# Loads of the down product's weights and of the logits' x placed later in the gate and up stage, and the head's first low parts in another order

## The chip, the cores and the metric

The kernel runs on one core of one Trainium2 chip. The metric is the time of an execution on the device, in microseconds (us). Before the change the median of three runs is 1020.63 us, and the three lie between 1020.56 and 1021.0. The profile comes from one further execution, which took 1021.83 us by itself; the span that the profile shows, from its first instruction to its last, is 1020.0 us.

## The reference

With x of 2048 positions and 640 features, all in 32-bit floats, the kernel computes two sublayers and mixes them by a gate per position:

```python
g = sigmoid((x * gate_w).sum(-1, keepdims=True))          # gate_w: 640
a = x @ dft_hid_re.T                                        # hidden DFT, 640 x 640
b = x @ dft_hid_im.T
y = dft_seq_re @ a - dft_seq_im @ b                         # sequence DFT, 2048 x 2048
ffn = (gelu(x @ w_gate) * (x @ w_up)) @ w_down              # F = 1728 hidden columns
out = g * y + (1 - g) * ffn
```

The arguments of the sigmoid, one per position, are called the logits below.

## The kernel before

**Products.** Every product of 32-bit floats is done as three matmuls of a shorter format: high x high, high x low and low x high (`mm3`, lines 101 to 103). For these ACT writes the high part of an operand (`high`, line 82) and DVE the low part as raw minus high (`low`, line 85). In the profile a name that ends in h or l is such a part. Most matrix products are also done blockwise: 2 x 2 blocks with seven products in place of eight, by sums of blocks of both operands. The sums of the weights are called S1 to S4, those of x T1 to T4.

**Stages.** The work goes through these stages, in this order:

- the *head*: the first 128 hidden columns (f = 0) and the 64 that are left over from 1728 = 13 x 128 + 64 ("m"), while x comes in piece by piece;
- the *gate and up stage*: twelve chunks of 128 hidden columns, f = 1 to 12, for which gelu(x w_gate) * (x w_up) is computed. "Chunk f" below is one turn of this loop;
- the *down stage*, the product with w_down, and behind it the sequence DFT, and last the hidden DFT with the gating.

**A chunk of the gate and up stage.** `gate_up` does a chunk's products for each half of the tokens. From chunk 3 on, two chunks make a pair: the odd one (3, 5, 7, 9, 11; kind 1 in the code) also does products that it shares with the even one behind it (kind 2), by a further level of blocks (`together` and `together_up`). The odd chunks take 30 us or more for this reason, the even ones some 17.6. `together` reads sums of x called T1 to T3, which were computed once and kept in memory; the loads that fetch them again for chunk f are called xq. `together_up` reads another such set, and its loads are called xu. Both are issued on POOL's queue (`load_across`, line 1150), the xu of an odd chunk within its first two steps, the xq in the fifth step of the chunk before. The gelu's results are stored to memory as blocks (hA) and sums of blocks (hT) by POOL (`keep`, line 404). In the odd chunks from 5 on, POOL also makes two of the weights' low parts, by a DMA that adds onto what stands in the buffer (`left_of`, line 97).

**Weights of the chunk.** Raw weights of chunk f + 2 are loaded in step 5 of chunk f (`load_w`). Their sums and parts for chunk f + 1 are made by work items of `make_w`: wa are the parts of the weights themselves, ws those of the sums of the chunk's own two columns of blocks, wq those of the sums across a pair. `make_up` makes the weights wu of `together_up` (its raw buffer is wu7r in chunk 7, its parts wu7h and wu7l).

**Two side works of the stage.** The first is the sums of w_down for the down stage: `sum_wd(k)` (line 606) loads a chunk's blocks as dr (512 KB) and da (128 KB) on SP's queue, makes four sums on DVE in two work items (lines 595 and 596, then 599 and 600) and stores them as wsd on SP's queue, behind the second item. Only the down stage reads wsd. The second is the logits: `load_z` (line 709) loads a tile of x, 128 positions by 640 features, as xz (320 KB, line 716), and a work item called a *total* multiplies it by gwb, the gate's weights, and sums it into one column of z on DVE (line 720). There are sixteen such tiles; the others are done elsewhere in the kernel. The gates of the first half of the tokens are made at chunk 12.

**What sets the order.** PE, ACT, DVE and POOL run the stage in exactly the order in which the host code emits the instructions (`in_order`). PE's steps are emitted as generators' steps, and the work of the other engines stands in one list, `fills`, of pairs (cost, function). After each step of PE the list is served so far as the spent costs stay within 1.25 times PE's share of the chunk:

```python
while fills and not (some and not fills[0][0]) and state["done"] <= 1.25 * state["all"] * state["pe"] / state["pe_all"]:
```

What is left is emitted at the end of the chunk. So the place of an item in `fills` and the costs ahead of it say when its instructions come on their engine. An engine that waits holds up all that stands behind it in its order. SP, which issues loads and a few stores, is not in this list of four engines, but its queue is served in its own order too.

**Buffers.** Most operands of the stage live in 46 equal buffers of one pool (tag s4, 4 KB on each of 128 partitions): weights raw and in parts, xq and xu, xz, dr, the gelu's blocks s. A new tile takes the buffer that has stood unused longest in the order of the code, and whoever fills it waits until the one who had it last is read out.

**Where the work stands before.** At the start of each odd chunk 5, 7, 9 and 11, right behind the loads of `make_up`, the code loads dr and da for a sum_wd and an xz; the two items of the sums stand early in the list, then follow a total in the middle, with it a second xz load, and a second total near the end; `make_w`'s items for the next chunk come last. In the even chunks 6 and 8 (`ZE_AT`) one xz is loaded at the start, and its total is the item at place 5. Chunk 3 (`PAIRED`) has a sum_wd and no total, chunk 12 a sum_wd of its own.

**The head.** For the first 128 rows of the contraction (d = 0) x's first piece x011 comes in two halves of 256 columns, and so do its parts and its products with the left-over columns' weights (w0h and w0l in the profile, wh and wl in the code, line 1051). PE, ACT and DVE are held in the code's order here as well.

Of the kernel before, what the change touches and what calls it, by code (L numbers as in the profile page):

```python
# [22 lines left out]
NF = F // P  # L23
# [4 lines left out]
EORD = [0, 2, 1, 3, 4]  # L28
PAIRED = 3
ZB_AT = [5,7,9,14,15,16]  # L30
ZE_AT = [6, 8]
XB_DOWN = [17, 18]
XB_AT = [1, 3, 4, 5, 9, 10]
WU_AT = [4, 17, 19, 33, 35]
# [3 lines left out]
def kernel(  # L38
# [45 lines left out]
    def low(hi, lo, raw):  # L84
        nc.vector.tensor_tensor(lo, raw, hi.bitcast(F32), op=ALU.subtract)  # L85
# [910 lines left out]
    halves = [slice(0, T // 2), slice(T // 2, T)]  # L996
# [22 lines left out]
    with in_order(ACT, DVE, PE):  # L1019
        nc.scalar.activation(table, table, AF.Gelu_apprx_tanh)  # L1020
        idle = bank("idle")
        for k in range(14):
            nc.tensor.matmul(idle[:, halves[k % 2]], *ones, start=k == 0, stop=True, skip_group_check=True)
        bk1, bk2 = first_banks(0, 1), first_banks(0, 2)
        for d in range(ND):
            raw, _, (h, l) = piece(d, 1)
            first, *rest = FIRST[d]
            parts(high, *first)
            if d == 0:
                a, b = halves  # L1030
                nc.vector.tensor_copy(h[:, a], raw[:, a])
                parts(low, *first)
                low(h[:, a], l[:, a], raw[:, a])
                split(h[:, b], l[:, b], raw[:, b])
                parts(high, *rest[0])
                parts(low, *rest[0])
            else:
                high(h, raw)
                parts(low, *first)
                low(h, l, raw)  # L1040
                for r in rest:
                    parts(high, *r)
                for r in rest:
                    parts(low, *r)
            split_piece(d, 2)
            if d == 0:
                wh, wl = W0["m"][0]
                for c in halves:
                    for k, (w, x) in enumerate(((wh, h), (wl, h), (wh, l))):
                        first = k == 0 and c is halves[0]  # L1050
                        nc.tensor.matmul(bk1["m"][:, c], w, x[:, c], start=first, stop=False, skip_group_check=True)
                for n in "gu":
                    mm3(bk1[n], W0[n][0], (h, l), True, False)
            else:
                first_products(bk1, W0, B, 1, [d])
            first_products(bk2, W0, B, 2, [d])
        B0, (tsum0, his0, lows0) = B, (tsum, his, lows)
        Bs.append(B)
        B, tiles, load, piece, tsum, his, lows = load_x(1)
        tiles(1)  # L1060
        load(1)
        tiles(2)
        load(2)
        tsum0(1)
        his((1, 1), (2, 1))
        lows((1, 1), (2, 1))
        split_piece(4, 1)
        first_out(bk1, 0, 1)
        first_out(bk2, 0, 2)
        bk1 = first_banks(1, 1)  # L1070
        first_products(bk1, W0, B, 1)
        tsum0(3)
        his0("T1", "T3")
        lows0("T1", "T3")
        tsum0(2)
        tsum0(4)
        his((1, 2), (2, 2))
        lows((1, 2), (2, 2))
        split_piece(4, 2)
        his0("T2", "T4")  # L1080
        lows0("T2", "T4")
        first_out(bk1, 1, 1)
        load_w(1)
        W, work = make_w(1)
        for _, do in work:
            do()
        load_w(2)
        nc.sync.dma_start(gwb, gw.to_broadcast([P, D]))
        bk2 = first_banks(1, 2)
        first_products(bk2, W0, B, 2)  # L1090
        tsum(1)
        his("T1")
        tsum(2)
        his("T2")
        lows("T1")
        first_out(bk2, 1, 2)

        todo.extend([(114, partial(lows, "T2")), (114, partial(tsum, 3)), (0, partial(his, "T3"))])
        todo.extend([(114, partial(tsum, 4)), (0, partial(his, "T4"))])
        todo.extend([(114, partial(lows, "T3")), (114, partial(lows, "T4"))])  # L1100
# [52 lines left out]
    fills, state = deque(), {}  # L1153
# [15 lines left out]
            fill(ns)  # L1169
            next(steps)  # L1170

    s1t, s4 = {}, {}
    Tp.update(B11=at(Bs[0][2, 1], 0), B21=at(Bs[0][2, 1], 1), B22=at(Bs[1][2, 1], 1))
    blocks = [("11", xt[0, 2]), ("12", xt[2, 2]), ("22", xt[2, 3]), ("21", xt[0, 3])]
    keptp, loadp, t123, t4 = sums_across("xp", Tp, blocks, lambda: at(Bs[1][2, 1], 0))
# [2 lines left out]
    with in_order(PE, ACT, DVE, POOL):  # L1178
        for f in range(1, NF):
            kind = pair_of(f)  # L1180
# [5 lines left out]
            if kind == 1:  # L1186
                up, work = make_up(f, load_up(f))
                fills.extend(work)
            if kind == 1:
                lw, *w = sum_wd((f - PAIRED) // 2)  # L1190
                lw[1]()
                fills.extend(w)
            if f == PAIRED - 1:
                loadp()
                fills.extend(t123)
# [6 lines left out]
                if kind != 1 or f == PAIRED:  # L1202
                    fills.extend(work)
            if kind == 1 and f > PAIRED:
                (_, first), z1, (_, second), z2 = load_z(2)
                first()
                k = len(fills) // 2
                more = list(fills)
                fills.clear()
                fills.extend([*more[:k], z1, (0, second), *more[k:], z2, *work])  # L1210
            elif f in ZE_AT:
                (_, first), z1 = load_z(1)
                first()
                fills.insert(5, z1)
            if f == NF - 1:
                load_k(0)
                fills.extend(split_pieces(0))
# [481 lines left out]
```

## Time and profile before

| of the profile before | |
| --- | --- |
| median of three runs (lowest, highest) | 1020.63 us (1020.56, 1021.0) |
| the profiled execution's own time | 1021.83 us |
| its span | 1020.0 us |
| PE busy | 1015.6 us, 4483 matmuls |
| PEld busy | 840.2 us |
| DVE busy | 823.2 us |
| ACT busy | 486.1 us |
| POOL busy | 166.9 us |
| DMA, mean over the span | 262 GB/s |
| granted clock of TensorE | 1.0 |

PE is TensorE's matmuls, PEld its weight loads, which run beside the matmuls; DVE is VectorE, ACT ScalarE, POOL GpSimd, SP SyncE. A row of a timeline gives the start in us from the span's start, the length of the instruction, the engine (SPq is a load or store on SP's queue), the line of the code, the operation, what it writes and what it reads, the shapes, and in square brackets how long the engine stood before it and what released it. A row of the windows gives a stretch, its length, the busy time of PE, PEld, DVE, ACT and POOL with the number of instructions, and then the granted clock, the share of time in which the DMA engines were busy, and their GB/s. "To landing" is the time from the issue of a DMA to its end.

The chunks of the gate and up stage start on PE at these times of the profiled execution: chunk 3 at 95.4 us, 4 at 125.6, 5 at 143.2, 6 at 173.2, 7 at 190.85, 8 at 221.4, 9 at 239, 10 at 269.1, 11 at 286.7, 12 at 316.8, and the stage ends at 334.3.

### The profile page before, as it was taken

Reading aid. Unit: us, or ns where it says so; the run is one execution under the profiler, and the core shown is the slowest. Engines: PE = TensorE matmul, PEld = TensorE weight load, DVE = VectorE, ACT = ScalarE, POOL = GpSimd, SP = SyncE. Lnnn points to the kernel's source line nnn. Section 1 sums busy time; section 2 is a strip of 40 time slices with the busy share of each in tenths; the row PEclk is TensorE's granted clock in tenths of the full one; section 3 lists DMA queues with packets and bytes.
Section 4 is the critical chain, followed back from the end, with each engine's and each line's share of the span. In section 5 each row is a group of like instructions: output and inputs, shape, how many; then the busy total and the mean of one; then the engine's idle time right before and its main releaser. Section 6 shows DMA issues by size and latency. Waiting matters only on the chain.

```text
span 1020.0 us, 13269 instructions
## 1 busy us (share of the span) xinstructions
PE 1015.6 (100%) x4483; PEld 840.2 (82%) x4483; DVE 823.2 (81%) x1154; ACT 486.1 (48%) x622; POOL 166.9 (16%) x295
## 2 busy tenths in 40 slices
PE   9999999999999999999999999999999999999998
PEld 7888888888888888888888888888888888888887
DVE  6987877787787989888887976898588869797796
ACT  5544534353535667557444443444344444455440
POOL 0122242323231200100001012102210200021112
PEclk9999999999999999999999999999999999999999
DMA  7468588968699999979874669668866877897856
GB/s 271 168 209 276 181 264 275 314 225 290 201 315 313 415 374 383 330 245 329 295 254 172 213 223 337 223 200 298 302 203 209 294 252 275 295 349 215 274 134 99
DMA packets 96644, 267.58 MB, mean 262 GB/s; under 512 B 12672, under 2 KB 27008, under 8 KB 96576
## 3 DMA queue, kind: packets, MB, share of 16 engines
q1 hardware_dynamic: 70512, 185.24, 53.2%
q0 software_dynamic: 25776, 81.30, 24.4%
q8 instruction: 35, 0.57, 0.2%
q14 instruction: 33, 0.27, 0.1%
q10 hardware_dynamic: 288, 0.20, 0.1%
HBM read 192.48 MB, written 70.27 MB: 258 GB/s over the span
## 4 chain that ended last, share of the span: by engine, by line
PE 97%; issue 1%; DMA 1%; DVE 0%; POOL 0%; POOLq 0%
PE pX L103 6%; PE pX L102 6%; PE pX L101 6%; PE pZ L103 4%; PE pZ L102 4%; PE pZ L101 4%; PE pL L102 3%; PE pL L103 3%; PE pL L101 3%; PE pV L102 2%; PE pV L103 2%; PE pV L101 2%; PE pY L102 1%; PE pR L103 1%; PE pQ L101 1%; PE pQ L102 1%
## 5 line engine op out<-in xcount | busy, mean ns | idle before, releaser
L82 ACT ACTIVATE ch<-csa 128x1024 fp32r<-128x1024 f32 x32 | 34.0, 1063 | 78.2 <-DVE csa L770 76.7
L85 DVE TENSOR_TENSOR cl<-cra,ch 128x1024 fp32r<-128x1024 f32 x32 | 39.1, 1222 | 24.6 <-ACT ch L82 22.5
L82 ACT ACTIVATE ch<-cra 128x1024 fp32r<-128x1024 f32 x32 | 33.9, 1059 | 52.3 <-DVE cl L85 19.3
L85 DVE TENSOR_TENSOR cl<-crb,ch 128x1024 fp32r<-128x1024 f32 x32 | 39.1, 1223 | 14.4 <-ACT ch L82 14.4
L102 PE MATMUL pL<-cl,xah 128*128 128x512 f32 x128 | 49.9, 390 | 0.0
L103 PE MATMUL pL<-ch,xal 128*128 128x512 f32 x128 | 49.9, 390 | 0.0
L101 PE MATMUL pL<-ch,xah 128*128 128x512 f32 x128 | 49.7, 390 | 0.0
L82 ACT ACTIVATE ch<-crb 128x1024 fp32r<-128x1024 f32 x32 | 33.8, 1055 | 31.2 <-PE pL L102 11.4
L404 POOL DMA_DIRECT2D hA<-s x48 | 26.1, 544 | 132.7 <-DVE s L562 113.1
L85 DVE TENSOR_TENSOR cl<-csb,ch 128x1024 fp32r<-128x1024 f32 x32 | 39.2, 1225 | 3.7 <-ACT ch L82 2.3
L85 DVE TENSOR_TENSOR cl<-csa,ch 128x1024 fp32r<-128x1024 f32 x32 | 39.1, 1221 | 2.1 <-ACT ch L82 1.1
L82 ACT ACTIVATE ch<-csb 128x1024 fp32r<-128x1024 f32 x32 | 34.0, 1062 | 11.7 <-DVE csb L773 4.7
L556 ACT ACTIVATE s<-s 128x512 f32<-128x512 f32 x24 | 15.2, 633 | 46.7 <-DVE s L555 46.7
L148 ACT ACTIVATE s<-pX 128x512 f32<-128x512 f32 x40 | 23.5, 598 | 23.7 <-PE pX L103 22.4
L85 DVE TENSOR_TENSOR kl<-kw,kh 128x1024 fp32r<-128x1024 f32 x24 | 29.4, 1223 | 4.5 <-DMA kw<-in_wd 2.6
L82 ACT ACTIVATE kh<-kw 128x1024 fp32r<-128x1024 f32 x24 | 25.3, 1052 | 16.1 <-PE kR L103 6.2
L551 DVE TENSOR_TENSOR s<-s,pX 128x512 f32<-128x512 f32 x24 | 16.5, 686 | 19.6 <-PE pX L103 14.3
L1346 POOL DMA_DIRECT2D uA<-c x8 | 4.3, 542 | 168.9 <-DVE c L1448 168.7
L404 POOL DMA_DIRECT2D hT<-s x48 | 26.0, 541 | 24.3 <-DVE s L579 8.1
L929 POOL DMA_DIRECT2D out<-ks x12 | 6.5, 541 | 136.8 <-DVE ks L928 136.2
L101 PEld LDWEIGHTS pL<-ch,xah 128*128 128x128 f32 x128 | 24.0, 188 | 5.0
L102 PEld LDWEIGHTS pL<-cl,xah 128*128 128x128 f32 x128 | 24.0, 188 | 5.0
(3612 smaller groups left out, 3483.8 us busy)
## 6 DMA issues: line engine op xcount, KB each, us to landing
cra<-in_ct SPq DMA_DIRECT2D x64, 512.0 KB, 4.6
crb<-in_ct SPq DMA_DIRECT2D x64, 512.0 KB, 5.0
hA<-s POOLq DMA_DIRECT2D x48, 256.0 KB, 5.9
hT<-s POOLq DMA_DIRECT2D x48, 256.0 KB, 5.7
kr<-hA SPq DMA_DIRECT2D x24, 512.0 KB, 7.7
kr<-hT SPq DMA_DIRECT2D x24, 512.0 KB, 6.8
ux<-uA SPq DMA_DIRECT2D x24, 512.0 KB, 5.9
ux<-uT SPq DMA_DIRECT2D x16, 512.0 KB, 6.7
```

Of the source, the lines that this page charges most:

```text
L82: nc.scalar.activation(hi, raw, AF.Copy)
L85: nc.vector.tensor_tensor(lo, raw, hi.bitcast(F32), op=ALU.subtract)
L101: nc.tensor.matmul(ps, lh, rh, start=first, stop=False, skip_group_check=True)
L102: nc.tensor.matmul(ps, lh, rl, start=False, stop=False, skip_group_check=True)
L103: nc.tensor.matmul(ps, ll, rh, start=False, stop=last, skip_group_check=True)
L148: nc.scalar.activation(m, src, AF.Copy)
L404: nc.gpsimd.dma_start(to[:, i], src)
L551: tt(s5, s5, X, op=ALU.add)
L556: nc.scalar.activation(s2, s2, AF.Gelu_apprx_tanh)
L929: nc.gpsimd.dma_start(acc4[:, t] if tp and e == 4 else out[2 * tp + t, e], src)
L1346: nc.gpsimd.dma_start(to[:, i], src)
```

## The change

It has three parts.

- **The sums of w_down.** In chunks 5, 7, 9 and 11 the loads of dr and da no longer stand at the chunk's start; the load is now an item of cost 0 in `fills`, behind what stood there and ahead of `make_w`'s items, and the two items of the sums stand behind the first five of `make_w`'s. Chunks 3 and 12 stay as they are.
- **The logits.** The odd chunks 5, 7, 9 and 11 load no xz at their start and do no total. Each even chunk 4, 6, 8 and 10 loads two xz at its start, with their totals put into the list at places 9 and 12. Chunks 7 and 9 (`ZE_AT` now) issue one further xz load at the end of their list, and its total is put at place 4 of the list of the chunk behind, 8 and 10. So the even chunks have 2, 2, 3 and 3 totals, and the sum stays at ten.
- **The head.** For d = 0, DVE makes the low part of the first half of x ahead of the first weights' low part, and PE does the products of that half in the order (high, high), (weights high, x low), (weights low, x high). The second half's order stays.

```diff
-ZE_AT = [6, 8]
+ZE_AT = (7, 9)
@@ head, d == 0 @@
                 nc.vector.tensor_copy(h[:, a], raw[:, a])
+                low(h[:, a], l[:, a], raw[:, a])
                 parts(low, *first)
-                low(h[:, a], l[:, a], raw[:, a])
                 split(h[:, b], l[:, b], raw[:, b])
...
                 for c in halves:
-                    for k, (w, x) in enumerate(((wh, h), (wl, h), (wh, l))):
+                    order = ((wh, h), (wl, h), (wh, l)) if c is halves[1] else ((wh, h), (wh, l), (wl, h))
+                    for k, (w, x) in enumerate(order):
                         first = k == 0 and c is halves[0]
                         nc.tensor.matmul(bk1["m"][:, c], w, x[:, c], start=first, stop=False, skip_group_check=True)
@@ gate and up stage @@
-    s1t, s4 = {}, {}
+    s1t, s4, zlate = {}, {}, []
...
             if kind == 1:
                 lw, *w = sum_wd((f - PAIRED) // 2)
-                lw[1]()
-                fills.extend(w)
+                if f == PAIRED:
+                    lw[1]()
+                    fills.extend(w)
...
             if kind == 1 and f > PAIRED:
-                (_, first), z1, (_, second), z2 = load_z(2)
-                first()
-                k = len(fills) // 2
-                more = list(fills)
-                fills.clear()
-                fills.extend([*more[:k], z1, (0, second), *more[k:], z2, *work])
-            elif f in ZE_AT:
-                (_, first), z1 = load_z(1)
-                first()
-                fills.insert(5, z1)
+                fills.extend([lw, *work[:5], *w, *work[5:]])
+                if f in ZE_AT:
+                    fetch, z1 = load_z(1)
+                    fills.append(fetch)
+                    zlate.append(z1)
+            elif kind == 2 and f < NF - 1:
+                if zlate:
+                    fills.insert(4, zlate.pop())
+                for k in (9, 12):
+                    (_, do), z1 = load_z(1)
+                    do()
+                    fills.insert(k, z1)
```

## The prediction

> **What bounds the kernel now.** I read the page's span and busy rows first, then the engines' busy time by windows, then the chain of waits in order of time for the places where it leaves TensorE, and last the timelines around the one such place that the change touches. The page:
>
> ```profile
> span 1020.0 us, 13269 instructions
> PE 1015.6 (100%) x4483; PEld 840.2 (82%) x4483; DVE 823.2 (81%) x1154; ACT 486.1 (48%) x622; POOL 166.9 (16%) x295
> ```
>
> Busy time by windows (the window, its length, then the busy time of PE, PEld, DVE, ACT and POOL):
>
> ```profile
> 0.00:10.00 10.00, 9.22 (x37) 6.97 (x38) 4.02 (x10) 5.24 (x10) 0.20 (x4) 1.00 0.82 256
> 190.00:240.00 50.00, 49.88 (x220) 40.84 (x219) 37.88 (x74) 22.25 (x37) 14.22 (x25) 1.00 0.79 262
> 940.00:1020.00 80.00, 76.48 (x349) 63.69 (x347) 64.38 (x86) 26.50 (x31) 12.74 (x15) 1.00 0.71 175
> ```
>
> PE is the bound. It idles 0.78 us in the first window, 0.12 in the second and 3.52 in the last, around its last matmul; these three are the whole 4.4 us between span and busy time. So what a new order of loads can gain is capped at PE's few late starts, while a new wait of PE costs its full length. The one late start in the gate and up stage, in the chain of waits and on PE's timeline:
>
> ```profile
> 207.69 5.28 DMA xu<-xv
> 213.01 0.50 PE pH7u L101
> ```
>
> ```profile
> 212.27 0.39 PE L102 MATMUL pX<-xT03l,ws7h 128*128 128x512 f32 x1
> 212.50 0.39 PE L103 MATMUL pX<-xT03h,ws7l 128*128 128x512 f32 x1
> 213.01 0.50 PE L101 MATMUL pH7u<-xu,wu7h 128*128 128x512 f32 x1
> 213.34 0.40 PE L102 MATMUL pH7u<-xu,wu7h 128*128 128x512 f32 x1
> ```
>
> Undisturbed matmuls start 0.23 us apart (212.27 to 212.50). The start at 213.01 comes 0.51 after the one before it, and the next 0.33 after that: 0.28 + 0.10 = 0.38 us lost in chunk 7, because its second xu load (the kept sum T2) landed only then, 207.69 + 5.28 = 212.97. Why it was issued so late, on POOL, on DVE and on SP's queue:
>
> ```profile
> 202.58 0.55 POOL L1150 DMA_DIRECT2D xu<-xv  x1 [0.30 <-issue]
> 207.69 1.14 POOL L1150 DMA_DIRECT2D xu<-xv  x2 [4.56 <-DVE dr L595]
> ```
>
> ```profile
> 202.20 0.83 DVE L720 CUSTOM_DVE_ANT_0 xz<-xz,gwb 128x640 f32<-128x640 f32 x1 [3.64 <-DMA hT<-s]
> ...
> 206.46 0.82 DVE L85 TENSOR_TENSOR wu7l<-wu7r,wu7h 128x640 fp32r<-128x640 f32 x1 [0.57 <-DMA hT<-s]
> 207.20 0.42 DVE L595 TENSOR_TENSOR dr<-da,dr 128x256 f32<-128x256 f32 x1
> ```
>
> ```profile
> 191.04 0.62 SPq L612 DMA_DIRECT2D dr<-in_wd  x1
> 192.44 3.05 SPq L716 DMA_DIRECT2D xz<-in_xz  x2
> ```
>
> POOL was ready for this load at 203.1 and stood 4.56 us: the load takes over the buffer of wu7r, which DVE reads until 207.28 (206.46 + 0.82). The row names dr's sum as the releaser, but that had only begun at 207.20; the wu7l just ahead of it is what ends in time. DVE was late in turn, because it had stood 3.64 us in front of the total of an xz, and 0.57 us for a buffer that an hT store still held. The DMA view of 190.8 to 204 us, and one row of the same view for 125.6 to 143 us, where SP loads little:
>
> ```profile
> DMA packets 1737, 4.91 MB, mean 372 GB/s; under 512 B 253, under 2 KB 509, under 8 KB 1736
> ...
> hT<-s POOLq DMA_DIRECT2D x6, 256.0 KB, 7.6
> ...
> xz<-in_xz SPq DMA_DIRECT2D x2, 320.0 KB, 9.2
> dr<-in_wd SPq DMA_DIRECT2D x1, 512.0 KB, 8.3
> ```
>
> ```profile
> hT<-s POOLq DMA_DIRECT2D x2, 256.0 KB, 2.4
> ```
>
> The start of chunk 7 is thus a queue of transfers: a store that lands in 2.4 us elsewhere takes 7.6 here, an xz 9.2.
>
> **The change part by part.** *Chunks 5, 7, 9 and 11, their start.* SP no longer loads dr (512 KB) and two xz (320 KB each) there: 1152 KB or 1.18 MB, at 372 GB/s 3.2 us of transfer that the stores and xu no longer queue behind. Both totals leave DVE's order in these chunks. Without the 3.64 us, and without the 0.57 us (with two or three fewer takers ahead of it wu7l gets a buffer that came free earlier), wu7l starts at 206.46 - 4.21 = 202.25 and ends at 203.1, just when POOL comes to the load. How long xu takes, in the view of that tile:
>
> ```profile
> L1150 POOL DMA_DIRECT2D xu<-xv x12: 537/548/551, 154.6 to 302.6; - x12
> ...
>   DVE dr L595: 12.9, 3
> ...
> DMA to landing us min/median/max: 5.2/5.6/6.4
> ```
>
> At the longest, 6.4, T2 lands at 209.5, 3.5 us before PE wants it. The three waits of 12.9 us in all are those of POOL in chunks 5, 7 and 9; only the one in chunk 7 reached PE. The gain is 0.38 us, with ends of 0 (something else is late) and 0.38. I take 0.38, since 3.5 us of margin stand behind it.
>
> *Chunks 4, 6, 8 and 10.* They hold 2, 2, 3 and 3 totals where 0, 1, 1 and 0 stood. DVE's idle stretches in these four, in their order:
>
> ```profile
> 136.98 0.29 DVE L85 TENSOR_TENSOR wd<-wb,wd 128x128 fp32r<-128x128 f32 x1 [3.31 <-ACT wd L82]
> ...
> 185.68 0.69 DVE L551 TENSOR_TENSOR s<-s,pX 128x512 f32<-128x512 f32 x1 [1.65 <-ACT s L547]
> ...
> 233.81 0.69 DVE L551 TENSOR_TENSOR s<-s,pX 128x512 f32<-128x512 f32 x1 [3.58 <-ACT s L547]
> ...
> 280.47 0.29 DVE L85 TENSOR_TENSOR wd<-wb,wd 128x128 fp32r<-128x128 f32 x1 [3.31 <-ACT wd L82]
> ```
>
> A total takes DVE 0.83 us (the row at 202.20). What is added is 1.66, 0.83, 1.66 and 2.49 us against 3.31, 1.65, 3.58 and 3.31 idle, and these stretches lie behind the places where the totals go in: cost 0, covered by that idle time; were it gone, DVE would be late with ws of the next chunk by as much. A total must not stand for its landing. By the code's budget the totals come 8.2 to 10.2 us into the chunk, their loads at its start, so at the slowest landing (9.2) DVE stands about 1 us, which the same idle time takes up; the third xz of chunks 8 and 10 goes out at the end of the chunk before. What can suffer is the chain to xq, the T1 with which the next chunk opens; chunk 6 is the tightest:
>
> ```profile
> 185.39 0.57 POOL L1150 DMA_DIRECT2D xq<-xp  x1 [2.08 <-DMA wa7l<-wa7r]
> ...
> 191.53 0.39 PE L101 MATMUL pZ7t<-xq,wq7h 128*128 128x512 f32 x1
> ```
>
> ```profile
> DMA to landing us min/median/max: 3.8/5.0/7.0
> ```
>
> 185.39 + 5.0 leaves 1.1 us; at 7.0 PE would wait 0.9. One more xz is 0.9 us of transfer at 372 GB/s. The ends are 0 and 0.9; I take 0, as the xz go out some 12 us ahead of xq.
>
> A rule that speaks against this part: the Trainium skill, SBUF — State Buffer, section "Who interferes with whom", says that a vector instruction with both inputs in SBUF and a GpSimd one that reads SBUF exclude each other for the whole of whichever began first. If that holds for the descriptors of POOL's DMAs, totals beside its accumulating DMAs delay these, and the sum would be that of the third rival. The trace does not bear it out: the xu issue at 202.58 lay wholly beside a total (202.20 to 203.03) and took 0.55, as did the median of the twelve, 0.548; so by the row the sum stays.
>
> *The weights' sums in chunks 5, 7, 9 and 11.* The code's budget (costs of 1103 in all, spent at 1.25 times PE's share of the chunk) takes up dr's load 12.9 us into the chunk and its sums at 19.0 and 21.8; SP sends the load as soon as its buffer is free. What the buffer may wait for, and the matmul that DVE's sums may hold up:
>
> ```profile
> 207.06 1.08 ACT L537 ACTIVATE s<-pZ 128x512 f32<-128x512 f32 x2 [1.67 <-DMA hT<-s]
> ```
>
> ```profile
> 219.26 0.39 PE L101 MATMUL pH7u<-xT14h,wu7h 128*128 128x512 f32 x1
> ```
>
> The buffer is free at the latest with the last hT store, about 207.0; with the slowest dr, 8.3, it lands at 215.3. Until then DVE stands at the first sum. Queued behind it are the other three sums of 0.42 and three additions of 0.69 (two of pX, one of pH7u), after which PE may overwrite pH7u at 219.26: 4 x 0.42 + 3 x 0.69 = 3.75, so 219.05. The worst case just fits, by 0.2 us. With the stores up to 3.2 us sooner and 5.6 us for the load (the median of xu, of the same size) dr is there at 209.4, and the sums' place, 190.85 + 19.0 = 209.9 (chunk 7 starts one matmul group, 0.68 us, ahead of the 191.53 above), is not held up. Cost 0; what comes beyond is the slower rival. On SP the four wsd stores follow the sums, and the loads of chunk 9's weights stand behind them; chunk 8 lies between, so some us of delay are covered, and wsd is read only in the down stage. Cost 0.
>
> *Head.* x's first low half no longer stands behind w's low part on DVE, and PE takes it second in the first half.
>
> ```profile
> 3.69 0.58 PE L1051 MATMUL pm<-x011h,w0h 128*128 128x256 f32 x1
> ...
> 4.73 0.42 PE L1051 MATMUL pm<-x011h,w0h 128*128 128x256 f32 x1
> ...
> 7.64 0.51 PE L102 MATMUL pm<-x012l,w0h 128*128 128x512 f32 x1
> ```
>
> ```profile
> 6.23 0.63 ACT L82 ACTIVATE x012h<-xr 128x512 fp32r<-128x512 f32 x1 [1.76 <-DMA xr<-in_xt]
> ```
>
> The first half's three products take 1.04 us (3.69 to 4.73); the overlap of DVE's two parts could shorten that by the 0.29 to 0.38 that one of them takes, I estimate 0.3. But at 7.64 PE starts on the low part of x012, whose chain begins with a landing at 6.23 that the change does not touch (0.63 for the high part, then DVE's low part). What is won ahead is waited for there: 0, with 0.3 as the other end; I take 0, as the wait ends in a transfer.
>
> **Sum.** -0.38 us: span 1019.6, and this execution, 1021.83, becomes 1021.45. It lies 1.2 us above the median of the runs, to which the difference applies as well: 1020.63 - 0.38 = 1020.25. PE has no idle time between chunk 7 and its last matmul, so the gain is carried to the end whole.
>
> **The rivals.** (1) The stall stays, or one of its size takes its place: T2's buffer or POOL is late for another reason. For it: POOL works in strict order behind ten stores, and PE has little slack in these chunks. Against: 3.5 us of margin. 1020.6. (2) xq is late in chunk 6, up to +0.9: 1021.15. For: 1.1 us of margin and one xz more; against: those 12 us. (3) The totals hold POOL's accumulating DMAs: two in chunk 6, 1.66 - 1.1 = 0.6, and three in chunk 10, taken with the same margin, 2.49 - 1.1 = 1.4; +2.0, 1022.25. Against: the 0.55 of the row. (4) Slower: dr is late. From a landing past 215.5 in chunk 7 on DVE, and with it PE, is held us for us, and likewise in 5, 9 and 11; with one us past that point in each it is +4, 1024.25. For: these loads are given their buffers in turn, and the turn now comes after stores' buffers. Against: it takes the slowest store and the slowest load seen, with 1.18 MB less ahead of them. (5) The head's 0.3 comes through: 1019.95.
>
> **How the numbers follow.** The forecast has 0.63, the rivals 0.13, 0.11, 0.03, 0.07 and 0.03. About 0.2%, 2 us, is what a measurement of this kernel can tell from no change; only (4) lies beyond, and no case reaches 1018.6; for what I have not seen 0.01 stands there. So slower 0.07, within 0.92, faster 0.01. The range holds the forecast, (1), (2) and (5) with the 0.4 us by which the runs shown differ: 1019.8 to 1021.3; (3) and (4) are left out.
>
> **What would show it.** Right: pH7u starts 0.23 us after the matmul before it; the second xu of chunk 7 goes out near 203 to 205; the hT stores at the start of chunks 5, 7, 9 and 11 land in 5 us or less; at the head a longer gap ahead of 7.64. Wrong: DVE stands in front of dr's sum (L595) until dr lands and PE waits at pH7u; or PE waits at pZ7t for xq; or the second xu goes out at 207 as before.

## The result, and the profile after

The changed kernel takes 1022.10 us in the median of 22 executions (1020.63 to 1029.34), the kernel before 1021.11 (1020.45 to 1022.62, 22 executions). The ratio is 1.0021 with a 95% interval of 1.0012 to 1.0030: about 0.2% slower, where 0.04% faster was forecast. The forecast of 1020.25 stood on a median of three executions, 1020.63; over 22 the kernel before is at 1021.11, so 0.48 us of the distance come from that base and the rest from the change, 0.99 us slower in place of 0.38 faster. The spread says more than the median. None of these 22 executions of the kernel before lies above 1023; of the changed kernel eight in 22 do, and all eight lie between 1024.5 and 1029.3. Six of the eight show a mean granted clock of 0.996 to 0.998 in place of 1.0.

The profile shown was taken of an execution of 1021.19 us, on the fast side. The page:

```profile
span 1019.4 us, 13283 instructions
PE 1014.5 (100%) x4483; PEld 839.0 (82%) x4483; DVE 822.8 (81%) x1154; ACT 487.2 (48%) x622; POOL 167.2 (16%) x295
```

Busy time by windows, the first two of before and one more:

```profile
0.00:10.00 10.00, 9.10 (x41) 6.96 (x42) 5.27 (x13) 6.45 (x14) 0.20 (x4) 1.00 0.80 278
190.00:240.00 50.00, 50.00 (x222) 41.36 (x221) 38.38 (x75) 22.81 (x38) 14.87 (x26) 1.00 0.81 267
285.00:300.00 15.00, 14.47 (x64) 11.65 (x63) 13.19 (x26) 4.78 (x8) 5.97 (x11) 1.00 1.00 345
```

PE's idle time of 0.12 us between 190 and 240 is gone, as forecast. A new one of 0.53 stands between 285 and 300, where PE was busy throughout before. PE's timeline at the old place and at the new one:

```profile
211.51 0.39 PE L103 MATMUL pX<-xT03h,ws7l 128*128 128x512 f32 x1
211.74 0.39 PE L101 MATMUL pH7u<-xu,wu7h 128*128 128x512 f32 x1
...
285.26 0.39 PE L101 MATMUL pH11t<-x021h,wa11h 128*128 128x512 f32 x1
...
288.44 0.39 PE L103 MATMUL pV11t<-x05h,wa11l 128*128 128x512 f32 x1
289.35 0.50 PE L101 MATMUL pH11t<-xq,wq11h 128*128 128x512 f32 x1 [0.53 <-DMA xq<-xp]
```

pH7u now starts 0.23 us after the matmul ahead of it. But at 289.35 PE starts 0.91 after the one ahead, 0.68 late, on the second xq load (the kept sum T2 for chunk 11). So 0.38 us are won and 0.68 lost in this execution. Its span is 0.6 us shorter than before all the same, because PE is already 0.95 us ahead when chunk 7 starts (189.90 against 190.85): in the head the first matmuls of full width ran 0.43 us apart before (from 5.37) and run 0.23 apart after (from 5.24), and x's second piece landed by 5.31 in place of 6.23. That belongs to the single execution and not to the order: of the profiles below f4, with the new order, has these matmuls 0.43 apart and f3, with the old one, 0.23. In other executions the new wait is longer. POOL's timeline, with the issue of the DMA that adds into wq11l and of the xq loads, first after, then before:

```profile
277.59 0.86 POOL L97 DMA_DIRECT2D wq11l<-wq11r  x1 [3.67 <-DMA wa11l<-wa11r]
278.41 0.60 POOL L1151 DMA_DIRECT2D xq<-xp  x1
283.55 0.56 POOL L1151 DMA_DIRECT2D xq<-xp  x1 [4.54 <-DMA wq11l<-wq11r]
```

```profile
278.24 0.86 POOL L97 DMA_DIRECT2D wq11l<-wq11r  x1 [2.92 <-ACT wq11l L93]
279.52 0.56 POOL L1150 DMA_DIRECT2D xq<-xp  x1 [0.42 <-issue]
283.43 1.24 POOL L1150 DMA_DIRECT2D xq<-xp  x2 [3.35 <-DMA wq11l<-wq11r]
...
286.66 0.39 PE L101 MATMUL pH11t<-x021h,wa11h 128*128 128x512 f32 x1
```

The second xq load takes the buffer of wq11r, which the adding DMA still reads. Measured from the first matmul of chunk 11, the adding DMA is issued 7.67 us ahead (285.26 - 277.59) in place of 8.42 (286.66 - 278.24), 0.75 later; its transfer takes 5.6 us in place of 4.8; so the second xq goes out 1.71 us ahead in place of 3.23. It then runs into the next weights' loads and lands after 5.8 us, 0.6 too late. (The adding DMAs that make the weights' low parts of the odd chunks 5, 7, 9 and 11 are issued one chunk ahead of each.) The row after names the landing of wa11l as the releaser, but ACT's activation L93, which prepares wq11l, ends 0.44 us ahead of the issue in both profiles (276.21 + 0.94 = 277.15, and 276.86 + 0.94 = 277.80), so the chain runs through it. Where the 0.75 comes from, on DVE, after and before:

```profile
273.01 0.68 DVE L525 TENSOR_TENSOR s<-s,pX 128x512 f32<-128x512 f32 x1
273.61 0.81 DVE L720 CUSTOM_DVE_ANT_0 xz<-xz,gwb 128x640 f32<-128x640 f32 x1
274.36 0.08 DVE L720 DVE_READ_ACCUMULATOR2_ANT z<- 128x1 f32 x1
274.36 0.28 DVE L291 TENSOR_TENSOR wq11r<-wa11r,wq11r 128x128 f32<-128x128 f32 x1
```

```profile
274.41 0.68 DVE L525 TENSOR_TENSOR s<-s,pX 128x512 f32<-128x512 f32 x1
275.01 0.29 DVE L291 TENSOR_TENSOR wq11r<-wa11r,wq11r 128x128 f32<-128x128 f32 x1
```

The third total of chunk 10, at place 4 of the list, stands between the sums that make wq11r. From L525 to L291 it takes 1.35 us in place of 0.60: 0.75 more, exactly the delay of the adding DMA. DVE itself has idle time for it, but only later in the chunk; ACT, POOL and the transfers that hang on wq11r leave DVE's order ahead of that idle time.

### The profile page after: what moved, and what is told of

It is laid out like the page before. It is cut to its first block, busy times and chain, and to the rows that moved or that the text cites. A ratio compares the mean times of both kernels' runs of the same rounds, so it can differ in the third digit from the quotient of the medians.

```text
span 1019.4 us, 13283 instructions
## 1 busy us (share of the span) xinstructions
PE 1014.5 (100%) x4483; PEld 839.0 (82%) x4483; DVE 822.8 (81%) x1154; ACT 487.2 (48%) x622; POOL 167.2 (16%) x295
## 4 chain that ended last, share of the span: by engine, by line
PE 94%; issue 3%; DMA 1%; POOL 1%; DVE 0%; ACT 0%; SPq 0%; POOLq 0%
PE pX L102 6%; PE pX L101 6%; PE pX L103 6%; PE pZ L102 4%; PE pZ L103 4%; PE pZ L101 4%; PE pL L101 3%; PE pL L103 3%; PE pL L102 3%; PE pV L101 2%; PE pV L103 2%; PE pV L102 2%; PE pR L103 1%; PE pQ L103 1%; PE pY L103 1%
## 5 line engine op out<-in xcount | busy, mean ns | idle before, releaser
L537 ACT ACTIVATE s<-pZ 128x512 f32<-128x512 f32 x24 | 14.2, 595 | 30.2 <-PE pZ L103 29.2
L103 PEld LDWEIGHTS pL<-ch,xal 128*128 128x128 f32 x128 | 24.0, 188 | 5.0
```

The costliest lines, as they stand in the source:

```text
L103: nc.tensor.matmul(ps, ll, rh, start=False, stop=last, skip_group_check=True)
L537: nc.scalar.activation(s5, Z, AF.Copy)
```

## The experiments

Two theories stood behind the first ones, with a rival X. T: the third total delays the chain wq, adding DMA, second xq, at chunk 10 (and less at 8). D: dr, loaded later, lands late, DVE stands for it, and PE with DVE. X: the bare number of xz loads ahead of the xq loads makes these late. "Late start" is the start of a matmul after the one ahead, less 0.23 us, in the profiled execution; its own time is in brackets. All were timed beside the kernel before (median 1021.1 to 1021.3, none above 1023.3).

| run | median us (lowest, highest), executions | ratio [95% interval] | late starts in the gate and up stage, us |
| --- | --- | --- | --- |
| e1, changed kernel again | 1022.07 (1020.74, 1025.35), 12 | 1.0010 [1.0002, 1.0019] | pH11t 0.15 (1020.74) |
| e2, third total last | 1033.52 (1032.94, 1034.15), 4 | 1.0118 [1.0103, 1.0132] | pX 3.0, 3.9 and 0.6 (1033.95) |
| e3, weights' sums alone | 1022.39 (1020.61, 1028.12), 12 | 1.0019 [1.0005, 1.0033] | pH7t 1.2 (1022.48) |
| e4, totals alone (with the head) | 1022.53 (1020.17, 1024.04), 11 | 1.0010 [1.0000, 1.0019] | pH11t 1.1 and 0.7 (1024.04) |
| f1, third total at place 7 | 1021.89 (1020.20, 1025.55), 12 | 1.0006 [0.9995, 1.0016] | none (1021.20) |
| f2, wq11l by DVE | 1020.96 (1020.63, 1026.61), 12 | 1.0006 [0.9995, 1.0017] | none (1020.83) |
| f3, head undone | 1022.17 (1020.86, 1027.32), 11 | 1.0011 [1.0000, 1.0022] | pH7t 1.0, pH11t 0.6 (1023.97) |
| f4, head alone | 1020.91 (1020.27, 1022.29), 11 | 0.9999 [0.9990, 1.0007] | none (1021.11) |
| h1, sums early, third total at 7 | 1021.13 (1020.65, 1021.66), 11 | 1.0000 [0.9991, 1.0009] | none (1020.89) |
| h2, load early, sums late, third at 7 | 1020.91 (1020.13, 1021.29), 11 | 0.9996 [0.9987, 1.0004] | pH7t 0.33 (1021.29) |
| h3, no adding DMA for wq | 1020.90 (1020.66, 1021.22), 11 | 0.9997 [0.9988, 1.0006] | none (1021.22) |
| h4, SP's queue delayed | 1025.40 (1023.65, 1027.65), 5 | 1.0043 [1.0030, 1.0056] | pX 0.5, pZ7t 1.8, pH7t 1.1 (1025.40) |
| k1, h2 and h3 together | 1021.07 (1020.26, 1021.47), 11 | 0.9998 [0.9989, 1.0007] | none (1021.16) |
| k2, SP's queue delayed twice | 1031.94 (1030.92, 1033.72), 4 | 1.0105 [1.0091, 1.0119] | pX 6.1, pZ7t 2.1 (1033.72) |

**The changed kernel again, and its parts.** e1 is the changed kernel as it is.

> The changed kernel once more, for its spread and for another profile. Theory T (the third total, put ahead of the sums across the pair, delays the accumulating DMA for wq11l by about 0.8 us in chunk 10, the second xq load waits for that DMA's buffer, and PE waits at pH11t): median near 1022, with single executions from 1024 to 1029, and in the profile a late start at pH11t of 0.5 us or more; nothing of that kind elsewhere. Rival D (dr lands late and holds DVE, then PE at pH5u, pH7u, pH9u or pH11u): same times, but the late starts stand at those products. Rival C (chance: the spread has nothing to do with the change): median 1021.1, no execution above 1023.

The median came again, and part of the spread: one execution of twelve lies above 1024, where eight of 22 did, and none shows a lower clock. The profiled execution was the shortest of the twelve, and its late start is 0.15, smaller than expected. So the spread lies between executions of one program, and the profile of a short one shows little of it.

```diff
-                if zlate:
-                    fills.insert(4, zlate.pop())
                 for k in (9, 12):
...
                     fills.insert(k, z1)
+                if zlate:
+                    fills.append(zlate.pop())
```

> The changed kernel with one edit: in chunks 8 and 10 the third total is the last item of the list in place of the fifth. Theory T: the stall at pH11t goes, median 1020.3 to 1021.2, no execution above 1023. Rival D (dr late) and rival X (the bare number of xz loads ahead of the xq loads): as the changed kernel, median near 1022 with executions above 1024.

This missed, and told neither theory from the other: 12 us slower. The third total had another use, which I had not seen. By its place it freed xz's buffer just ahead of the sums ws9r, which took that buffer. With the total at the end ws9r got the buffer of wq9r, and DVE waited for the adding DMA that reads it (DVE, then PE):

```profile
235.94 0.43 DVE L277 TENSOR_TENSOR ws9r<-wb,wa9r 128x256 f32<-128x256 f32 x1 [7.06 <-DMA wq9l<-wq9r]
...
241.70 0.80 PE L101 MATMUL pX<-x05h,wa 128*128 128x512 f32 x1 [2.85 <-DVE s L551]
```

Moving an item in this list moves buffers too.

e3 is the kernel before with dr's load and its sums late, the xz as they were; e4 the changed kernel with dr's part undone:

```diff
 e3, beside the same condition on f == PAIRED as in the change:
-                k = len(fills) // 2
+                k = len(fills) - 3
...
-                fills.extend([*more[:k], z1, (0, second), *more[k:], z2, *work])
+                fills.extend([*more[:k], z1, (0, second), *more[k:], z2, lw, *work[:5], *w, *work[5:]])
 e4:
-                if f == PAIRED:
-                    lw[1]()
-                    fills.extend(w)
+                lw[1]()
+                fills.extend(w)
...
-                fills.extend([lw, *work[:5], *w, *work[5:]])
+                fills.extend(work)
```

> The kernel before with one part of the change: dr's load and its sums stand later in chunks 5, 7, 9 and 11, the xz and their totals stay where they were. Theory T: 1020.7 to 1021.3, like the kernel before. Rival D: 1022 or more, with executions above 1024 and late starts of PE behind dr's sums. Rival X: like the kernel before.

> The changed kernel with dr's load and its sums put back to the start of chunks 5, 7, 9 and 11; the xz, their totals and the head stay changed. Theory T: median near 1022 with executions above 1024, and a late start at pH11t. Rival D: 1020.3 to 1021.2. Rival X: near 1022.

Each part alone costs about as much as both: neither theory had that, and X had e3 like the kernel before. e4 shows T's wait at pH11t; e3 shows a wait at pH7t, on the landing of the second xq that chunk 6 loads. DVE did stand 3.48 us for dr in chunk 5 of e3, but PE stood for a load and not for DVE, so D as put does not hold.

**One cause at a time.** f1 puts the third total behind the sums across and ACT's two parts of wq, but ahead of ws, so that every tile keeps its buffer. f2 makes wq11l by DVE's subtraction in place of ACT's negation and the adding DMA.

```diff
 f1:
-                    fills.insert(4, zlate.pop())
+                    fills.insert(7, zlate.pop())
 f2, in neg_q and in low_q:
+            if f == 11:
+                return
...
-            if f > PAIRED:
+            if f > PAIRED and f != 11:
                 left_of(q[1][:, 1:], rq[:, 1:])
```

> The changed kernel with the third total of chunks 8 and 10 at place 7 of the list in place of 4: behind the sums across the pair and ACT's two parts of wq, still ahead of the sums ws, so that every tile keeps its buffer. Theory T: the DMA that adds into wq11l is issued some 0.8 us sooner before the end of chunk 10 on PE (7.2 us in place of 6.5), the second xq load as much sooner, and the late start at pH11t goes or falls below 0.2 us: median 1020.5 to 1021.3. Rival Y (the xq loads land late for the traffic around them, not for their issue): pH11t still starts late, median near 1022.

> The changed kernel with wq's low part of chunk 11 alone made by DVE's subtraction in place of ACT's negation and POOL's adding DMA, so that no xq load of chunk 10 waits for that DMA's buffer (one DMA and one activation fewer, one subtraction of some 1.1 us more on DVE). Theory T: the second xq load goes out 3 us or more sooner, no late start at pH11t, median 1020.5 to 1021.3; if executions above 1024 remain, their cause lies at another chunk, 6 to 7 the likeliest. Rival Y: pH11t late as before. Rival D (dr holds DVE): near 1022, late starts at pH5u to pH11u.

POOL in f1, and PE:

```profile
277.67 0.86 POOL L97 DMA_DIRECT2D wq11l<-wq11r  x1 [2.92 <-DVE ws11r L282]
279.36 0.56 POOL L1151 DMA_DIRECT2D xq<-xp  x1 [0.83 <-DVE wb L296]
282.80 0.55 POOL L1151 DMA_DIRECT2D xq<-xp  x1 [2.87 <-DMA wq11l<-wq11r]
...
286.09 0.39 PE L101 MATMUL pH11t<-x021h,wa11h 128*128 128x512 f32 x1
```

The adding DMA is issued 8.42 us ahead of chunk 11 again, the second xq 3.29, and the late start at pH11t is gone: T's mechanism is shown. In every profile with the third total at place 4 and the adding DMA in use (the changed kernel, e1, e4, f3) this lead is 7.67, and in those without that total there (before, e3, f1) 8.42. But both runs keep two executions in twelve above 1024 (to 1025.6 and 1026.6), and f1's median of 1021.89 misses what T alone expected. Something else was left, and f3 caught it. It is the changed kernel with the three edits of the head reversed, and f4 the kernel before with these edits alone:

> The changed kernel with the head as it was. All theories of the gate and up stage: 0 to 0.3 us slower than the changed kernel, 1022.1 to 1022.4, with the same spread and the late start at pH11t. Rival H (PE's earlier start out of the head eats the margin of the loads): nearer to 1021.

> The kernel before with the head's part alone. Prediction on record: no change, as the start at the low part of x's second piece hangs on a transfer: 1021.1. Rival: 0.3 us come through, 1020.8. If rival H holds, 1021.5 or more.

By its times the head is neutral, alone and in the changed kernel; 0.2 us on the median of f4 is less than can be told. Rival H, which had f3 nearer to 1021, does not hold. The profile of f3 (SP's queue, DVE, then PE) shows the second cause:

```profile
156.17 0.33 SPq L612 DMA_DIRECT2D dr<-in_wd  x1
163.46 0.33 SPq L602 DMA_DIRECT2D wsd<-dr  x1
...
168.37 0.33 SPq L218 DMA_DIRECT2D wa7r<-in_wf  x1
...
163.00 0.43 DVE L595 TENSOR_TENSOR dr<-da,dr 128x256 f32<-128x256 f32 x1 [2.88 <-DMA dr<-in_wd]
...
194.65 0.39 PE L103 MATMUL pV7t<-x05h,wa7l 128*128 128x512 f32 x1
195.88 0.50 PE L101 MATMUL pH7t<-xq,wq7h 128*128 128x512 f32 x1 [0.84 <-DMA xq<-xp]
```

SP's queue in the changed kernel's own profile:

```profile
153.66 0.33 SPq L612 DMA_DIRECT2D dr<-in_wd  x1
158.91 0.33 SPq L602 DMA_DIRECT2D wsd<-dr  x1
...
163.22 0.33 SPq L218 DMA_DIRECT2D wa7r<-in_wf  x1
```

There dr landed 3.8 us after its issue. In f3 it goes out 2.5 us later (PE is 1.6 us later itself), lands after 6.7 us, and DVE stands 2.88 us for it in chunk 5. The wsd stores leave from 163.46, and wa7r's load, which takes dr's own buffer, at 168.37, 5.15 us later than in the changed kernel's profile, or 3.6 against PE. All that stands behind it on SP, two xz loads among it, now goes out in one bunch. The last of it, wb and da, goes out between 175.22 and 177.70 and lands 6.3 to 7.5 us later, when wa7l's adding DMA (issued at 179.67) is on its way; before, the first wb left at 172.41 and da at 172.88, and both had landed, after 5.1 and 5.0, ahead of that DMA (178.86); only a second wb went later, at 184.43. The DMA view from 176 to 192 us, f3 and then before:

```profile
xq<-xp POOLq DMA_DIRECT2D x3, 512.0 KB, 6.4
wa7l<-wa7r POOLq DMA_DIRECT2D x1, 512.0 KB, 7.2
wq7l<-wq7r POOLq DMA_DIRECT2D x1, 448.0 KB, 6.0
...
da<-in_wd SPq DMA_DIRECT2D x1, 128.0 KB, 6.3
wb<-in_wf SPq DMA_DIRECT2D x1, 128.0 KB, 7.5
```

```profile
xq<-xp POOLq DMA_DIRECT2D x3, 512.0 KB, 5.0
wa7l<-wa7r POOLq DMA_DIRECT2D x1, 512.0 KB, 5.9
wq7l<-wq7r POOLq DMA_DIRECT2D x1, 448.0 KB, 4.5
```

The adding DMAs are issued as far ahead of chunk 7 as before (wq7l 8.42 us in both), but land later, so the second xq load goes out with 1.5 us less lead on pH7t, and itself takes 6.4 us in place of 4.8, with the loads of the next weights going out behind it at 190.09: 3.1 us against a margin of 2.1. This is theory Q: dr late, wsd late, the next weights' loads late behind them, and the transfers of chunk 6 with them. Before, dr had landed more than 7 us ahead of its sums, and its lateness could not show.

**Q taken away, and doubled.** h1, h2 and h4 stand on f1. h1 puts load and sums of dr back to the start; h2 only the load; h3 is the changed kernel with wq's low parts of all four odd chunks by DVE; h4 adds sixteen stores of one column, emitted behind the wsd stores of chunk 5, to a scratch that nobody reads (in its profile four of them go out ahead of the wsd stores and twelve behind). Rival W, against Q: the second xz of chunk 6 is what makes its xq load late.

```diff
 h2:
-                if f == PAIRED:
-                    lw[1]()
-                    fills.extend(w)
+                lw[1]()
+                if f == PAIRED:
+                    fills.extend(w)
...
-                fills.extend([lw, *work[:5], *w, *work[5:]])
+                fills.extend([*work[:5], *w, *work[5:]])
 h4, in sum_wd, for k == 1:
                      last()
+                    for q in range(16):
+                        nc.sync.dma_start(probe[:, q : q + 1], r[:, q % 8, q // 8 : q // 8 + 1])
```

> Totals and head as changed, the third total at place 7, dr's load and its sums back at the start of chunks 5, 7, 9 and 11. Theory Q (where dr lands late, the wsd stores leave SP's queue late, the loads of the next weights stand behind them and run into chunk 6, the adding DMAs and the second xq load of chunk 6 land late, and PE waits at pH7t): with the sums early the stores leave by 157, wa7r's load by 164 in every execution; with the third total out of the way too no late start at pH7t or pH11t above 0.2 us, median 1020.4 to 1021.0, no execution above 1023. Rival W (the second xz of chunk 6 is what makes its xq load late): late starts at pH7t stay, with executions above 1024.

> As the run with the third total at place 7, with one more edit: dr's load stands at the chunk's start, its sums stay late, so dr can't be late for them. Theory Q: wsd stores leave at the place of the sums, near 158 in every execution, wa7r by 164; median 1020.5 to 1021.2, no execution above 1024. Rival W: as that run, median near 1022 with executions above 1024.

> The changed kernel with wq's low parts of chunks 5, 7, 9 and 11 made by DVE in place of the adding DMA, so that no xq load waits for one. Theories T and Q: both late starts go, since the second xq load no longer waits for a transfer: median 1020.3 to 1021.0, no execution above 1023. If DVE has not the 1.1 us to spare in chunk 10 (three totals): a late start behind ws11l instead.

> As the run with the third total at place 7, with sixteen stores of one column each (512 bytes, to a scratch that nobody reads) behind the wsd stores of chunk 5 on SP's queue: nothing else is delayed, SP's queue by some 7 us. Theory Q: wa7r's load leaves at 168 or later in every execution, wa7l, wq7l and the second xq load land late, pH7t starts 0.8 us or more late; median 1022.5 to 1026, with half of the executions or more above 1023. Rival W, or a cause on DVE: no change against that run, 1021.9.

With both causes taken away, h1, h2 and h3 have no execution above 1021.7, and the excess is gone: 1020.9 to 1021.1 (h1 lies 0.1 above what was expected). All three keep the xz loads of the change, so neither X nor W accounts for the excess. h2 keeps the sums late and has no execution above 1021.3, so it is the load that mattered: in its profile wa7r's load leaves at 163.20. Its median is 1.0 us below f1's for that one edit, and eight of f1's twelve executions lie above every one of h2's. Its profile still has 0.33 us at pH7t, with wa7r's load on time, so the margin there stays thin; what takes it is not shown. h3 leaves dr as late as it was (in its profile wa7r's load leaves at 167.28) and frees the xq loads from the adding DMA: the second xq of chunk 6 goes out at 186.15 and lands 4.7 us later, 3.2 us ahead of PE's use at 194.14. So the lateness cost time by way of the adding DMA; h3 takes away its hold on the buffer and its 448 KB of transfer together, and does not tell them apart. In h4, which delays SP's queue alone, and with it the release of dr's buffer (SP's queue, then PE):

```profile
164.12 6.77 SPq L622 DMA_DIRECT2D probe<-dr  x12
171.06 0.33 SPq L219 DMA_DIRECT2D wa7r<-in_wf  x1
...
194.24 0.50 PE L101 MATMUL pZ7t<-xq,wq7h 128*128 128x512 f32 x1 [1.68 <-DMA xq<-xp]
...
198.20 0.50 PE L101 MATMUL pH7t<-xq,wq7h 128*128 128x512 f32 x1 [0.95 <-DMA xq<-xp]
```

and the DMA view of 176 to 192 us of h4:

```profile
wa7l<-wa7r POOLq DMA_DIRECT2D x1, 512.0 KB, 9.1
wq7l<-wq7r POOLq DMA_DIRECT2D x1, 448.0 KB, 7.9
```

Every execution lies above 1023.6, though PE waits more for the first xq load (pZ7t) than for the second, which Q had named. Q is shown: by taking it away, by taking out the adding DMA it works through, and by doubling it.

**The executions with a lower clock.** The waits caught so far, up to 1.8 us, do not add up to 1026. k2 is h4 with thirty-two stores; k1 joins h2 and h3, to see whether all of the spread goes and whether that beats the kernel before.

> The two remedies together: dr's load at the chunk's start with late sums and the third total at place 7, and wq's low part made by DVE in place of the adding DMA in chunks 5, 7, 9 and 11. No load of the stage then waits for a late transfer: no late start in the stage at all, median 1020.5 to 1020.9, no execution above 1021.6; better than the changed kernel by 1.2 to 1.6 us, against the kernel before 0 to 0.6 us faster, about what can be told apart. If DVE has no time left for both (1.1 us a chunk more, beside the totals): late starts behind ws9l or ws11l, 1021.5 or more.

> As the run with sixteen small stores on SP's queue in chunk 5, with thirty-two: the queue some 7 us later again, the wait of PE at the xq loads of chunk 6 some 4 to 7 us instead of 2.6. If long waits of this kind account for the executions above 1024 with a lower granted clock, each execution here shows the lower clock, matmuls 0.43 us apart in place of 0.23 behind the wait for 2 to 4 us, and the time is 1030 to 1036. If the lower clock had another cause, matmuls 0.23 us apart directly behind the wait, and 1028 to 1032.

PE in k2, and a window of it:

```profile
187.03 0.80 PE L101 MATMUL pX<-xT12h,ws6h 128*128 128x512 f32 x1 [5.91 <-DVE s L526]
...
202.19 0.50 PE L101 MATMUL pZ7t<-xq,wq7h 128*128 128x512 f32 x1 [1.98 <-DMA xq<-xp]
...
202.99 0.62 PE L101 MATMUL pZ7t<-x15h,wq7h 128*128 128x512 f32 x1
203.40 0.63 PE L102 MATMUL pZ7t<-x15l,wq7h 128*128 128x512 f32 x1
...
206.39 0.40 PE L103 MATMUL pV7t<-x05h,wa7l 128*128 128x512 f32 x1
```

```profile
202.00:207.00 5.00, 4.81 (x14) 3.82 (x15) 3.81 (x7) 0.77 (x2) 2.25 (x5) 0.66 0.97 367
```

Behind an idle time of 1.98 us in front of an xq load, the matmuls from 202.99 to 206.39 start 0.43 us apart in place of 0.23: eight of them, 3.40 us in place of 1.82, so such a wait costs 1.6 us more than itself. The granted clock is 0.66 in that window, and all four executions show 0.995 to 0.998; the stretch behind the wait of 5.91 us has its part in these. In h4's profile the wait of 1.68 us was followed by starts 0.23 apart. The expectation was wrong on the size of the xq wait, since the longer delay first held chunk 6 itself (5.91 us at pX) and the xq wait behind it stayed at 2; the time fell into the expected range by this other wait. On the clock it held. No profile fell on an execution of the changed kernel with a lower clock, so that the same happens there rests on its mean clock and on k2: a mean of 0.998 over 1025 us is some 4 us at half clock, by estimate, about one such stretch. Which waits add up to 1026 or 1029 is not shown. k1 has no late start and nothing above 1021.5, but its median of 1021.07 misses the 1020.5 to 1020.9 expected, and against the kernel before it is not faster: no version found beats it by more than can be told.

## Why the prediction was wrong

- **The stall on xu in chunk 7: right.** The second xu goes out at 201.66, behind the end of wu7l at 201.26, POOL stands 1.34 us for it in place of 4.56, and pH7u is on time. The 0.38 us are there. The hT stores at the start of chunks 5, 7, 9 and 11 land in 4.4, 5.1, 4.1 and 5.8 us in the median, in place of 7.0, 7.6, 6.5 and 6.9; 5 or less was forecast, which two of the four meet.
- **The totals at cost 0: the first step that failed.** "[T]hese stretches lie behind the places where the totals go in: cost 0, covered by that idle time" is true of DVE and false of what leaves DVE's order ahead of that idle time. The text then named the right chain, xq, but for the wrong chunk, for the first of the three loads in place of the second, and for the wrong reason (a further xz to transfer). Chunks 8 and 10 have a total inside the sums of wq, 0.75 us on ACT, POOL and two transfers in a row. That no total stands for its landing was right: in the groups by line, from 118 to 335 us, the ten have no idle time in front of them.

```profile
L720 DVE CUSTOM_DVE_ANT_0 xz<-xz,gwb 128x640 f32<-128x640 f32 x10 | 8.2, 817 | 0.0
```

- **The weights' sums at cost 0: the second step that failed.** "On SP the four wsd stores follow the sums, and the loads of chunk 9's weights stand behind them; chunk 8 lies between, so some us of delay are covered". Chunk 8 does cover the weights themselves. It does not cover the transfers around them: where the same happened a pair earlier (sums in chunk 5, loads for chunk 7), ACT took up wa7r on time against PE (at 173.70 in f3, 173.06 before, with chunk 7 starting 0.63 later), but a shift of 3.6 us on SP against PE made the adding DMAs of chunk 6 land 1.3 and 1.5 us slower than before the change and cost PE 1.0. I asked whether the weights come in time, not what their loads collide with.
- **Rival 4, dr late.** Half right. DVE did stand for dr: 2.14 us in chunk 7 in the profile after, 2.88 in chunk 5 in f3. In chunk 7 that was not a late landing: dr came at 208.4, far ahead of the rival's 215.5, but DVE had reached the sums 16.3 us into the chunk in place of the 19.0 worked out. And PE was not held through DVE and pH7u; the way went through SP's queue, POOL's adding DMAs and xq, to the next odd chunk.
- **Rival 2, xq late, at 1021.15.** The right kind of wait, PE on an xq load, but put at the first load (pZ7t) of chunk 6; in the changed kernel and its parts PE waited for the second (pH7t, pH11t). It was sized 0.9 at most; measured were 0.6 to 1.2 in single profiles of e3, e4, f3 and the changed kernel, at either of two chunks, and, where a wait reached 1.98 us (k2), a lower clock behind it.
- **Rival 3, totals against POOL's DMAs.** Not borne out: the adding DMA of chunk 10 was issued at 277.59 while a total still ran (276.97 to 277.79) and took 0.86, as before with none beside it. The rule of the Trainium skill, SBUF — State Buffer, section "Who interferes with whom", was weighed there; no run here shows its effect on the issue of a DMA.
- **The head: right on the size, not on the sign.** No change that can be told. The longer gap ahead of the low part of x012 did not come: it starts 0.23 us after the matmul ahead of it in the profile after (6.85) and 0.24 in f4 (7.43). Where x's second piece landed late the start of its product waited, with the new order as with the old (8.29 in e4 and 8.31 in f3, landings at 6.88 and 6.90). The landing, which the change does not touch, moves by more than the 0.3 us in question.
- **The chances.** Slower by over 0.2% had 0.07. The rival that held it was priced as one mechanism with a far threshold. The range allowed for the 0.4 us by which three runs differed, while the 22 of the kernel before differ by 2.2. What was missed is that the change thins two margins, at pH7t from 2.1 us in the profile before to 1.6 in the one after and at pH11t from some 2.5 to none, and that these are drawn anew in every execution by transfers that vary by some 3 us (dr in chunk 5 took 3.8 to 7.1 in the profiles with the late load), so that the sum of a single profile's slacks was not a forecast of the median.

## What to carry to other kernels

Cover on an engine hides only what ends on that engine: for each item put ahead of others, follow the instructions that leave its order before the idle time comes, through other engines and DMAs to the one that PE reads. In this kernel a load that lands well ahead of its use kept a whole queue on time; taking it later to relieve a busy moment passed the variation of its landing on to every store and load behind it, and to whoever shares the bandwidth with those. When slacks are near the spread of a transfer's landing, look at several executions: the profile of the shortest execution of the changed kernel (e1) showed almost nothing.

## What the runs showed that was not expected

- Single executions of one program differ by up to 9 us (1020.6 to 1029.3) with these two margins thin, and by under 1.3 us (h3 1020.66 to 1021.22, h2 1020.13 to 1021.29) with the causes taken away; those of the kernel before by 2.2 (1020.45 to 1022.62).
- TensorE's clock fell around idle times of 1.98, 2.85, 3.77 and 5.91 us (k2, e2, e2, k2) and not behind 0.95, 1.05 and 1.68 (e4, e3, h4). Read from the granted clock of short windows (0.92 in 185.50:186.00 of k2, 0.50 in 186.00:186.50), the stretches at half clock lie at 185.92 to 192.75 and 202.98 to 206.40 in k2, at 241.62 to 245.04 and 296.23 to 299.65 in e2: 3.42 us, once 6.83. The distances between these times within a profile are whole multiples of some 3.41 us. The Trainium skill, TensorE: Matmul & The Clock Gate, "Part 1: The HAM clock gate", gives a free-running window of about 3.4 us after which an idle array drops to half its clock. Length and grid agree; but the window of k2 that ends at 202.98 held only 1.98 us of idle time, and those of e2 before its drops no more than 2.8. So whether a wait of 2 us brings the lower clock may hang on where it falls in the grid; no run here varies that.
- An accumulating DMA of 448 KB took 4.5 us to land in chunk 6 before the change, and 6.0 and 7.9 with SP's loads shifted onto it (f3, h4).
- In a pool whose buffers are all taken, the order of work items decides which tile waits for which: one total moved by a few places cost 12 us (e2).
